# A causal convolution and a gated feed-forward layer: how the first x is loaded, how the taps are spread, and what TensorE does meanwhile

## The chip, the core and the metric

The kernel runs on one core of a Trainium2 chip. The metric is the device time of one execution in microseconds (us). The engines are TensorE (PE in the profile; PEld is its loading of stationary operands), VectorE (DVE), ScalarE (ACT), GpSimd (POOL) and SyncE (SP), which here issues transfers.

## The reference

`x` is 8 sequences of 4096 tokens with 192 channels. Each channel is convolved along the tokens with 7 taps; the channels fall into 8 heads of 24, and a head's taps are the softmax of its row of `weight`. The result goes through a feed-forward layer with a gate:

```python
w = weight - np.max(weight, axis=-1, keepdims=True)      # 8 heads x 7 taps
w = np.exp(w)
w = w / (np.sum(w, axis=-1, keepdims=True) + 1e-09)
x_pad = np.concatenate([np.zeros((B, pad, D), dtype=np.float32), x], axis=1)
idx = np.arange(S)[:, None] + np.arange(K)[None, :]
x_unf = x_pad[:, idx, :].reshape(B, S, K, H, group)
out = np.einsum('hk,bskhg->bshg', w, x_unf)              # 8 x 4096 x 192
...
gate = np.maximum(x @ w_gate, 0.0)                       # 192 -> 1536
val = x @ w_val
return (gate * val @ w_out).astype(np.float32)           # 1536 -> 192
```

## The kernel before

The tokens are worked in 16 units of 1024 tokens of two streams (sequence b and sequence b + 4), which lie in the two halves of the partitions. For each unit the convolved x (`xc`, channels on partitions, three chunks of 64 channels) is multiplied with `Wg` and `Wv` in 12 steps of 128 columns (`gate_val`, L477, matmuls L490). ScalarE applies the ReLU (L499), VectorE the product (L500), and `project` multiplies with `Wo` (L519, L539) and writes the rows out (L552, L553). The convolution of units 2 to 15 runs on VectorE, ScalarE and GpSimd beside the matmuls of earlier units. That of units 0 and 1 is done on PE, as a product with banded matrices that hold the taps: `conv_dense` for the two windows of 512 tokens of unit 0, `conv` for unit 1. The change touches what comes before the first `gate_val`.

The order of each engine's instructions is that of the program (`manual_schedule`), so an instruction that waits holds all that are behind it on its engine.

**The first x.** A window has five steps (`GSUB`) of 104 tokens, with six earlier tokens each. SyncE loads the taps' logits `wr` (L104), then steps 1 to 4 of the first stream as fp32 (L125) and step 0 of both streams (L141) into `stage`, which is a view of a buffer that is used only later (`prods`). GpSimd loads steps 1 to 4 of the second stream with a cast to fp16 straight into the tile `xts[0]` (L130). ScalarE casts the staged steps 1 to 4 (L275), VectorE step 0 (L276).

**The weights.** GpSimd issues their transfers in slices (`load_w`, L173) with a cast, into partitions 0 to 63. `both_halves` copies a slice to partitions 64 to 127 (L180): VectorE does it for slices 0 and 1, GpSimd for the others. Between slices 2 and 3 GpSimd issues the x of the second window (L90).

**The taps and the band.** VectorE takes the maximum (L214), ScalarE exp (L217), VectorE the sum, the reciprocal and the taps in `w8`, each repeated 16 times (L219 to L222). A matmul with a piece of the identity (L232) brings them onto 112 partitions (`spread`), VectorE multiplies with `same` (L242), and 14 matmuls with shifted `places` (L253) make the banded matrices of the eight heads in two PSUM tiles. `same` and `places` are sums over `spaced` (L201), which GpSimd fills (L129, L131). VectorE copies heads 0 to 3 to `band0`, ScalarE heads 4 to 7 to `band4` (both L282). Ten small transfers on SyncE lay the taps out on the partitions (L269) for the later units; GpSimd copies them on (L605).

**Filling matmuls.** `warm_up` (L155) multiplies constants into a PSUM tile that nobody reads: six matmuls of 512 columns at the start and two after `spread`.

**The first convolution.** `conv_dense(0, c)` for the three chunks c (L599) does 40 matmuls each (L318) over all five steps and copies the chunk to `xc` (L328): chunk 1 by VectorE, chunks 0 and 2 by ScalarE. Chunk 0 needs heads 0 to 2, chunk 1 heads 2 to 5, chunk 2 heads 5 to 7. Three more calls, for the second window, lie in the first `gate_val` (L482).

Of the kernel before, what the change touches and what calls it, by code (L numbers as in the profile page):

```python
# [15 lines left out]
def kernel(  # L16
# [98 lines left out]

    xts[0] = xpool.tile([128, GSUB, 2, D], F16, name="x_h")

    def body(st):
        return bass.AP(
            tensor=x.tensor,  # L120
            offset=x.offset + (NB * st * S + DSUB - PAD) * D,
            ap=[[D, SUB], [DSUB * D, GSUB - 1], [1, D]],
        )
# [6 lines left out]
    nc.gpsimd.dma_start(out=xts[0][0:SUB, 1:GSUB, 1, :], in_=body(1))  # L130
# [24 lines left out]
    def warm_up(count):  # L155
        for n in range(count):
            nc.tensor.matmul(
                out=warm[:, n % 2, :], lhsT=busy[:, 0:128], rhs=busy, start=True, stop=True
            )

    warm_up(6)

# [23 lines left out]
    load_w(0)  # L186
    load_w(1)
    load_w(2)
    xts[1] = load_x(1)
    load_w(3)  # L190
    pool_halves(2)
    load_w(4, 6)
    pool_halves(3)
# [25 lines left out]
    nc.vector.tensor_reduce(out=sm[:], in_=ex[:], axis=mybir.AxisListType.X, op=ALU.add)  # L219
    nc.vector.reciprocal(sm[:], sm[:])  # L220
    w8 = const.tile([H, KW, SEG], FP)
    nc.vector.tensor_scalar(  # L222
        out=w8[:],
        in0=ex[:, 0:KW].unsqueeze(2).to_broadcast([H, KW, SEG]),
        scalar1=sm[:],
        scalar2=None,
        op0=ALU.mult,
    )
# [3 lines left out]
    nc.tensor.matmul(  # L232
        out=spread[0:SUB, 0, 0:H],
        lhsT=w8[:].rearrange("h k s -> h (k s)"),
        rhs=spaced[0:H, 0, GAP : GAP + H],
        start=True,
        stop=True,
    )
    warm_up(2)
    diag = const.tile([SUB, H, SEG], F16)  # L240
    with nc.allow_low_precision("products with one and zero"):
        nc.vector.tensor_tensor(  # L242
# [2 lines left out]
            in1=same[:].unsqueeze(1).to_broadcast([SUB, H, SEG]),  # L245
            op=ALU.mult,
        )
    summed(places[:, SUB - SEG : SUB - SEG + SEG + KW - 1], pitch_k - 1, SEG + KW - 1, GAP)
    bps = psum.tile([128, 2, 512], FP, name="ps")
    HB = H // 2  # L250
    for a in range(2):
        for b in range(NSEG):
# [6 lines left out]
                skip_group_check=True,  # L259
            )  # L260

    taps = const.tile([H, KW], FP)
    nc.scalar.copy(out=taps[:], in_=w8[:, :, 0])
    tap = const.tile([128, NCH, KW], FP)
    for h in range(H):
        r = G * h
# [5 lines left out]
            )  # L272
            r += n

    nc.scalar.copy(out=xts[0][0:ROWS0, 1:GSUB, 0, :], in_=stage(0, ROWS0, 0, 1, 1, GSUB - 1))  # L275
    nc.vector.tensor_copy(out=xts[0][0:ROWS0, 0, :, :], in_=stage(0, ROWS0, 0, 2, 0, 1))  # L276

    bands = []
    for a, copy in ((0, nc.vector.tensor_copy), (1, nc.scalar.copy)):
        part = const.tile([128, HB, SUB], F16, name=f"band{a}")  # L280
        bands += [part[0 : SUB + PAD, h, :] for h in range(HB)]
        copy(  # L282
            out=part[:].rearrange("p h (b s) -> p h b s", s=SEG),
            in_=(bps, spread)[a][:, a, 0 : HB * SUB].rearrange("p (b h s) -> p h b s", h=HB, s=SEG),
        )

    def band(h):
        return bands[h]

    xc = {}  # L290

# [5 lines left out]
    def conv_dense(g, c):  # L297


        xt = xts[g]  # L300
        if g == 0 and c == 0:
# [5 lines left out]
        ps = psum.tile([128, 2, 512], FP, name="ps")  # L307
        for jj in range(GSUB):
            col = DSUB * jj
            n = min(DSUB, WIN - col)  # L310
            for second in range(2):
                for st in range(2):
                    for k2 in range(2):
                        k = 2 * c + k2
                        h0, h1 = 32 * k // G, (32 * k + 31) // G
                        h, m = (h0, G * h1 - 32 * k) if second else (h1, 32)
                        p0 = 64 * st + 32 * k2
                        nc.tensor.matmul(  # L318
                            out=ps[p0 : p0 + m, 0, col : col + n],
                            lhsT=xt[0:rows, jj, st, 32 * k : 32 * k + m],  # L320
                            rhs=band(h)[0:rows, 0:n],
                            start=True,
                            stop=True,
                            tile_position=(0, p0),
                            skip_group_check=True,
                        )
        copy = nc.vector.tensor_copy if c == 1 else nc.scalar.copy
        copy(out=xc[0][:, c, t0 : t0 + WIN], in_=ps[:, 0, :])  # L328

# [147 lines left out]
    def gate_val(u, w):  # L477
        h = hpool.tile([128, NFF, 2, WIN], F16, name="hT")
        xcb = xc[u]
        for f in range(NFF):  # L480
            if u == 0 and w == 0 and f in (5, 7, 9):
                conv_dense(1, (f - 5) // 2)  # L482
            pss = [psum.tile([128, 2, 512], FP, name="ps") for _ in range(2)]
            order = [(i, c) for i in range(2) for c in range(NCH)]
            if u == 0 and w == 0 and f == 0:
                order = [(0, 0), (0, 1), (1, 0), (0, 2), (1, 1), (1, 2)]
            for i, c in order:
                W = (Wg, Wv)[i]
                for st in range(2):
                    nc.tensor.matmul(  # L490
                        out=pss[i][:, st, :],
                        lhsT=W[64 * st : 64 * st + 64, c, 128 * f : 128 * (f + 1)],
                        rhs=xcb[64 * st : 64 * st + 64, c, WIN * w : WIN * (w + 1)],
                        start=(c == 0),
                        stop=(c == NCH - 1),
                        tile_position=(64 * st, 0),
                    )
# [179 lines left out]
```

## Time and profile before

| | us |
|---|---|
| three runs | 769.77, 771.62, 771.74 |
| their median | 771.62 |
| the profiled execution | 769.56 |
| its span, from the first instruction to the last | 767.9 |
| busy: PE, VectorE, ScalarE, GpSimd | 761.8, 685.1, 604.1, 369.8 |
| first matmul of L490 | 8.10 |
| last matmul of L519 ends | 764.15 |

The profile is of one execution. Its page gives busy time by engine and by group of instructions; the trace behind it can be asked for all instructions in order of time, for the chain of waits (from the last instruction back to what released each step) and for transfers. A row of the timeline reads: start, length, engine, line, operation, output and inputs, shapes, how many, and in brackets how long the engine stood idle before it and what ended that.

### The profile page before, as it was taken

Reading aid. Unit: us, or ns where it says so; the run is one execution under the profiler, and the core shown is the slowest. Engines: PE = TensorE matmul, PEld = TensorE weight load, DVE = VectorE, ACT = ScalarE, POOL = GpSimd, SP = SyncE. Lnnn points to the kernel's source line nnn. Section 1 sums busy time; section 2 is a strip of 40 time slices with the busy share of each in tenths; the row PEclk is TensorE's granted clock in tenths of the full one; section 3 lists DMA queues with packets and bytes.
Section 4 is the critical chain, followed back from the end, with each engine's and each line's share of the span. In section 5 each row is a group of like instructions: output and inputs, shape, how many; then the busy total and the mean of one; then the engine's idle time right before and its main releaser. Section 6 shows DMA issues by size and latency. Waiting matters only on the chain.

```text
span 767.9 us, 24835 instructions
## 1 busy us (share of the span) xinstructions
PE 761.8 (99%) x10840; PEld 526.8 (69%) x10840; DVE 685.1 (89%) x728; ACT 604.1 (79%) x733; POOL 369.8 (48%) x212
## 2 busy tenths in 40 slices
PE   8999999999999999999999999999999999999998
PEld 4495675957759576585866858567595775957757
DVE  6999999989999999999999999999998999995590
ACT  6788887888878788887888878788787887874571
POOL 8608738093470925619166290843909346090000
PEclk9999999999999999999999999999999999999999
DMA  8946727180372704529064271712819231200102
GB/s 121 133 101 118 91 88 91 48 126 7 100 78 69 106 23 94 63 85 94 23 110 48 85 91 44 109 27 85 93 44 114 24 94 38 65 21 23 63 2 84
DMA packets 131809, 56.11 MB, mean 73 GB/s; under 512 B 96741, under 2 KB 131701, under 8 KB 131701
## 3 DMA queue, kind: packets, MB, share of 16 engines
q1 hardware_dynamic: 90789, 38.85, 24.3%
q0 software_dynamic: 40768, 15.59, 18.9%
q8 instruction: 84, 1.38, 0.8%
q14 instruction: 24, 0.20, 0.1%
q10 hardware_dynamic: 144, 0.10, 0.0%
HBM read 31.68 MB, written 25.17 MB: 74 GB/s over the span
## 4 chain that ended last, share of the span: by engine, by line
PE 99%; DMA 0%; DVE 0%; SPq 0%; issue 0%
PE ps L490 65%; PE ps L519 31%; PE ps L539 2%; DMA prods<-in_x_dram 0%; PE ps L318 0%; PE ps L343 0%; DVE xc L328 0%; DVE x_h L276 0%; DVE band L282 0%; SPq L104 0%; DVE acc L552 0%; SPq L125 0%
## 5 line engine op out<-in xcount | busy, mean ns | idle before, releaser
L500 DVE TENSOR_TENSOR hT<-gr,ps 128x1024 f16<-128x1024 f16 x384 | 468.4, 1221 | 59.9 <-ACT gr L499 32.2
L499 ACT ACTIVATE gr<-ps 128x1024 f16<-128x1024 f32 x384 | 393.0, 1023 | 100.5 <-PE ps L490 100.4
L443 POOL TENSOR_TENSOR prods<-prods 128x1344 f32<-128x1344 f32 x70 | 212.4, 3034 | 309.4 <-ACT out_s L552 279.3
L490 PE MATMUL ps<-xc,Wg 64*128 64x512 f16 x2304 | 317.3, 376 | 0.1
L490 PE MATMUL ps<-xc,Wv 64*128 64x512 f16 x2304 | 317.1, 376 | 0.0
L519 PEld LDWEIGHTS <-hT 64*128 64x128 f16 x5760 | 238.5, 94 | 3.1
L519 PE MATMUL ps<-Wo,hT 64*128 64x192 f16 x5760 | 240.3, 243 | 0.0
L490 PEld LDWEIGHTS <-Wv 64*128 64x128 f16 x2304 | 138.6, 94 | 111.0 <-issue 2.9
L490 PEld LDWEIGHTS <-Wg 64*128 64x128 f16 x2304 | 128.1, 94 | 116.6 <-issue 0.6
L466 DVE SCALAR_TENSOR_TENSOR acc<-x_r,tap,acc 128x576 f32<-128x576 f16 x210 | 154.3, 811 | 1.6 <-ACT acc L454 1.6
L437 ACT ACTIVATE prods<-x_r,tap 128x448 f32<-128x448 f16 x222 | 130.2, 660 | 1.2 <-DMA x_r<-x_p 1.2
L552 ACT COPY out_s<-ps 128x768 f32<-128x768 f32 x63 | 50.3, 799 | 53.1 <-PE ps L519 44.5
L399 POOL DMA_DIRECT2D x_e<-in_x_dram x56 | 45.2, 819 | 3.3 <-POOL x_p L418 3.3
L418 POOL COPY x_p<-x_e 128x1728 f16<-128x1728 f16 x28 | 44.7, 1621 | 2.4 <-DMA x_e<-in_x_dram 2.4
L443 POOL TENSOR_TENSOR xc<-prods 128x1344 f16<-128x1344 f32 x14 | 42.4, 3028 | 1.1
L466 DVE SCALAR_TENSOR_TENSOR xc<-x_r,tap,acc 128x576 f16<-128x576 f16 x42 | 31.8, 811 | 0.0
L454 ACT ACTIVATE acc<-x_r,tap 128x576 f32<-128x576 f16 x42 | 29.4, 767 | 0.0
L439 DVE TENSOR_SCALAR prods<-x_r,tap 128x448 f32<-128x448 f16 x72 | 27.3, 448 | 0.0
L539 PE MATMUL ps<-Wo,hT 128*128 128x192 f16 x192 | 16.2, 246 | 0.0
L539 PEld LDWEIGHTS <-hT 128*128 128x128 f16 x192 | 15.9, 98 | 0.0
L552 DVE COPY acc<-ps 128x192 f32<-128x192 f32 x1 | 0.4, 359 | 14.2 <-PE ps L519 14.2
L90 POOL DMA_DIRECT2D x_h<-in_x_dram x6 | 4.9, 826 | 0.0
(51 smaller groups left out, 56.4 us busy)
## 6 DMA issues: line engine op xcount, KB each, us to landing
out_dram<-out_s SPq DMA_DIRECT2D x63, 384.0 KB
x_e<-in_x_dram POOLq DMA_DIRECT2D x34, 192.0 KB, 6.6
x_e<-in_x_dram POOLq DMA_DIRECT2D x22, 240.0 KB, 6.3
x_r<-x_p SPq DMA_TRANSPOSE x126
Wo<-in_moe_w_out_dram POOLq DMA_DIRECT2D x1, 576.0 KB, 10.7
x_h<-in_x_dram POOLq DMA_DIRECT2D x2, 240.0 KB, 8.2
x_h<-in_x_dram POOLq DMA_DIRECT2D x2, 210.0 KB, 5.2
x_h<-in_x_dram POOLq DMA_DIRECT2D x2, 192.0 KB, 5.8
```

What stands on the lines that cost most here:

```text
L399: nc.gpsimd.dma_start(out=xe[:, j : j + n, st, :, :].rearrange("p j c r -> p j (c r)"), in_=bass.AP(tensor=x.tensor, offset=x.offset + (b ...
L418: nc.gpsimd.tensor_copy(out=xp[:, :, :, st, :], in_=xe[:, :, st, :, :])
L437: engine.activation(out=out, in_=in_, func=ACTF.Copy, scale=scale)
L443: nc.gpsimd.tensor_tensor(out=pr[:, 0] if k < KW - 1 else xc[u][:, :, LDVE:UNIT], in0=pr[:, 0], in1=pr[:, k], op=ALU.add,)
L454: nc.scalar.activation(out=accs[u][:, c, :], in_=shifted(u, c, 0, 0), func=ACTF.Copy, scale=tap[:, c, 0:1],)
L466: nc.vector.scalar_tensor_tensor(out=xc[u][:, c, 0:LDVE] if k == KW - 1 else acc[:, c, :], in0=shifted(u, c, k, 0), scalar=tap[:, c, k : k ...
L490: nc.tensor.matmul(out=pss[i][:, st, :], lhsT=W[64 * st : 64 * st + 64, c, 128 * f : 128 * (f + 1)], rhs=xcb[64 * st : 64 * st + 64, c, WI ...
L499: nc.scalar.activation(out=gr[:], in_=pss[0][:], func=ACTF.Relu)
L500: nc.vector.tensor_tensor(out=h[:, f], in0=gr[:], in1=pss[1][:], op=ALU.mult)
L519: mm = nc.tensor.matmul(out=outs[q], lhsT=h[64 * r : 64 * r + 64, f, st, 128 * q : 128 * (q + 1)], rhs=Wo[64 * r : 64 * r + 64, f, :], sta ...
L539: nc.tensor.matmul(out=outs[q], lhsT=h[:, f, st, 128 * q : 128 * (q + 1)], rhs=Wo[:, f, :], start=(f == 0), stop=(f == NFF - 1),)
L552: copy(out=dst, in_=src if len(src.shape) == 3 else src.unsqueeze(1))
```

## The change

- SyncE loads all of the first x as fp32: step 1 of both streams, step 0 of both streams, then steps 2 to 4 of the first and of the second stream. GpSimd's cast transfer is gone.
- GpSimd copies the maximum of the logits (`lead`) before it issues the first weights.
- exp writes each value 16 times at once, and is the stationary operand of the `spread` matmul as it is; the moving operand is the piece of the identity divided by the sum (`over`). `taps` is scaled by the reciprocal on ScalarE. The sum for `places` stands ahead of the product.
- VectorE copies the band in two parts (heads 0 to 2, head 3), ScalarE heads 4 to 7 as before. ScalarE casts step 1 of both streams, VectorE step 0; after the band ScalarE casts steps 2 to 4 of the first stream and VectorE those of the second.
- `conv_dense` for the first window runs in two rounds over the three chunks: steps 0 and 1, then steps 2 to 4.
- Filling matmuls: six of 512 columns and one of 128 at the start; 256 and 192 columns after `spread`; one of 512 after the 14 matmuls of the band.

```diff
-    nc.sync.dma_start(out=stage(0, SUB, 0, 1, 1, GSUB - 1), in_=body(0))
+    FEW = 2
+    rest = [DSUB * D, GSUB - FEW]
+    nc.sync.dma_start(out=stage(0, SUB, 0, 2, 1, 1), in_=body(1, [NB * S * D, 2]))
...
-    nc.gpsimd.dma_start(out=xts[0][0:SUB, 1:GSUB, 1, :], in_=body(1))
...
+    for st in range(2):
+        nc.sync.dma_start(
+            out=stage(0, SUB, st, 1, FEW, GSUB - FEW), in_=body(FEW, rest, st)
+        )
...
-    warm_up(6)
+    warm_up(512, 512, 512, 512, 512, 512, 128)
...
-    ex = const.tile([H, KW + 1], FP)
+    ex = const.tile([H, KW + 1, SEG], FP)
...
-    nc.scalar.activation(ex[:, 0:KW], wr[:], ACTF.Exp, bias=mx[:])
+    lead = const.tile([H, 1], FP)
+    nc.gpsimd.tensor_copy(out=lead[:], in_=mx[:])
+    load_w(0)
...
+    nc.scalar.activation(
+        ex[:, 0:KW, :], wr[:].unsqueeze(2).to_broadcast([H, KW, SEG]), ACTF.Exp, bias=mx[:]
+    )
...
-    w8 = const.tile([H, KW, SEG], FP)
+    over = const.tile([H, H], FP)
     nc.vector.tensor_scalar(
-        out=w8[:],
-        in0=ex[:, 0:KW].unsqueeze(2).to_broadcast([H, KW, SEG]),
+        out=over[:],
+        in0=spaced[0:H, 0, GAP : GAP + H],
         scalar1=sm[:],
...
     summed(same[:], pitch_k, SEG, GAP)
+    summed(places[:, SUB - SEG : SUB - SEG + SEG + KW - 1], pitch_k - 1, SEG + KW - 1, GAP)
...
-        lhsT=w8[:].rearrange("h k s -> h (k s)"),
-        rhs=spaced[0:H, 0, GAP : GAP + H],
+        lhsT=ex[:, 0:KW, :].rearrange("h k s -> h (k s)"),
+        rhs=over[:],
...
-    warm_up(2)
+    warm_up(256, 192)
...
-    summed(places[:, SUB - SEG : SUB - SEG + SEG + KW - 1], pitch_k - 1, SEG + KW - 1, GAP)
...
+    warm_up(512)
+
     taps = const.tile([H, KW], FP)
-    nc.scalar.copy(out=taps[:], in_=w8[:, :, 0])
+    nc.scalar.activation(taps[:], ex[:, 0:KW, 0], ACTF.Copy, scale=sm[:])
...
-    nc.scalar.copy(out=xts[0][0:ROWS0, 1:GSUB, 0, :], in_=stage(0, ROWS0, 0, 1, 1, GSUB - 1))
+    nc.scalar.copy(out=xts[0][0:ROWS0, 1, :, :], in_=stage(0, ROWS0, 0, 2, 1, 1))
...
+    fill_band(0, [0, 1, 2], nc.vector.tensor_copy)
+    fill_band(1, [4, 5, 6, 7], nc.scalar.copy)
+    fill_band(0, [3], nc.vector.tensor_copy)
+    nc.vector.tensor_copy(
+        out=xts[0][0:ROWS0, FEW:GSUB, 1, :], in_=stage(0, ROWS0, 1, 1, FEW, GSUB - FEW)
+    )
+    nc.scalar.copy(
+        out=xts[0][0:ROWS0, FEW:GSUB, 0, :], in_=stage(0, ROWS0, 0, 1, FEW, GSUB - FEW)
+    )
...
-    for c in range(NCH):
-        conv_dense(0, c)
+    pieces = [psum.tile([128, 2, 512], FP, name="ps") for _ in range(NCH)]
+    for steps in (range(FEW), range(FEW, GSUB)):
+        for c in range(NCH):
+            conv_dense(0, c, pieces[c], steps)
```

In the changed kernel the three new SyncE transfers of x stand in lines 127 and 149, `lead` in 214, VectorE's cast of steps 2 to 4 in 305, and the two rounds of the convolution use line 342 for its matmuls.

More of the change, by code (lines that the diff above doesn't have):

```diff
@@ L116, with body @@
     xts[0] = xpool.tile([128, GSUB, 2, D], F16, name="x_h")
-    def body(st):
+    def body(jj, step, st=0):
         return bass.AP(
             tensor=x.tensor,
-            offset=x.offset + (NB * st * S + DSUB - PAD) * D,
-            ap=[[D, SUB], [DSUB * D, GSUB - 1], [1, D]],
-        )
-    nc.sync.dma_start(out=stage(0, SUB, 0, 1, 1, GSUB - 1), in_=body(0))
+            offset=x.offset + (NB * st * S + DSUB * jj - PAD) * D,
+            ap=[[D, SUB], step, [1, D]],
+        )
+    FEW = 2
+    rest = [DSUB * D, GSUB - FEW]
+    nc.sync.dma_start(out=stage(0, SUB, 0, 2, 1, 1), in_=body(1, [NB * S * D, 2]))
     ones = const.tile([128, SUB], FP)
@@ L153, with warm_up @@
     warm = psum.tile([128, 2, 512], FP, name="ps")
-    def warm_up(count):
-        for n in range(count):
+    def warm_up(*widths):
+        for n, w in enumerate(widths):
             nc.tensor.matmul(
-                out=warm[:, n % 2, :], lhsT=busy[:, 0:128], rhs=busy, start=True, stop=True
+                out=warm[:, n % 2, 0:w], lhsT=busy[:, 0:128], rhs=busy[:, 0:w], start=True, stop=True
             )
-    warm_up(6)
+    warm_up(512, 512, 512, 512, 512, 512, 128)
     Wg = const.tile([128, NCH, DFF], F16)
@@ L184, in pool_halves @@
         both_halves(nc.gpsimd.tensor_copy, s, Wv)
[L186 to L193, printed above, removed]
-    ex = const.tile([H, KW + 1], FP)
+    ex = const.tile([H, KW + 1, SEG], FP)
     nc.vector.memset(ex[:], 1e-9)
@@ L216 @@
     )
-    nc.scalar.activation(ex[:, 0:KW], wr[:], ACTF.Exp, bias=mx[:])
+    lead = const.tile([H, 1], FP)
+    nc.gpsimd.tensor_copy(out=lead[:], in_=mx[:])
+    load_w(0)
+    load_w(1)
+    load_w(2)
+    xts[1] = load_x(1)
+    load_w(3)
+    pool_halves(2)
+    load_w(4, 6)
+    pool_halves(3)
+    nc.scalar.activation(
+        ex[:, 0:KW, :], wr[:].unsqueeze(2).to_broadcast([H, KW, SEG]), ACTF.Exp, bias=mx[:]
+    )
     sm = const.tile([H, 1], FP)
-    nc.vector.tensor_reduce(out=sm[:], in_=ex[:], axis=mybir.AxisListType.X, op=ALU.add)
+    nc.vector.tensor_reduce(out=sm[:], in_=ex[:, :, 0], axis=mybir.AxisListType.X, op=ALU.add)
     nc.vector.reciprocal(sm[:], sm[:])
-    w8 = const.tile([H, KW, SEG], FP)
+    over = const.tile([H, H], FP)
     nc.vector.tensor_scalar(
-        out=w8[:],
-        in0=ex[:, 0:KW].unsqueeze(2).to_broadcast([H, KW, SEG]),
+        out=over[:],
+        in0=spaced[0:H, 0, GAP : GAP + H],
         scalar1=sm[:],
@@ L273, with fill_band @@
             r += n
-    nc.scalar.copy(out=xts[0][0:ROWS0, 1:GSUB, 0, :], in_=stage(0, ROWS0, 0, 1, 1, GSUB - 1))
+    nc.scalar.copy(out=xts[0][0:ROWS0, 1, :, :], in_=stage(0, ROWS0, 0, 2, 1, 1))
     nc.vector.tensor_copy(out=xts[0][0:ROWS0, 0, :, :], in_=stage(0, ROWS0, 0, 2, 0, 1))
[L278 to L281, printed above, removed]
+    band_at = {}
+    def fill_band(a, heads, copy):
+        lo, n = heads[0] - HB * a, len(heads)
+        part = const.tile([128, n, SUB], F16, name=f"band{heads[0]}")
+        for i, h in enumerate(heads):
+            band_at[h] = part[0 : SUB + PAD, i, :]
         copy(
             out=part[:].rearrange("p h (b s) -> p h b s", s=SEG),
-            in_=(bps, spread)[a][:, a, 0 : HB * SUB].rearrange("p (b h s) -> p h b s", h=HB, s=SEG),
-        )
+            in_=(bps, spread)[a][:, a, 0 : HB * SUB].rearrange("p (b h s) -> p h b s", h=HB, s=SEG)[
+                :, lo : lo + n
+            ],
+        )
+    fill_band(0, [0, 1, 2], nc.vector.tensor_copy)
[7 more added lines that the diff above has]
+    )
     def band(h):
-        return bands[h]
+        return band_at[h]
     xc = {}
@@ L295, with conv_dense @@
     PLACE |= {6: (1, 0, 0), 7: (1, 0, 1), 2: (1, 1, 0), 5: (1, 1, 1)}
-    def conv_dense(g, c):
+    def conv_dense(g, c, ps, steps=range(GSUB)):
         xt = xts[g]
-        if g == 0 and c == 0:
+        if g == 0 and c == 0 and 0 in steps:
             xc[0] = xcpool.tile([128, NCH, UNIT], F16, name="xc")
@@ L306, in conv_dense @@
         rows = ROWS0
-        ps = psum.tile([128, 2, 512], FP, name="ps")
-        for jj in range(GSUB):
+        for jj in steps:
             col = DSUB * jj
@@ L326, in conv_dense @@
                         )
+        if GSUB - 1 not in steps:
+            return
         copy = nc.vector.tensor_copy if c == 1 else nc.scalar.copy
@@ L481, in gate_val @@
             if u == 0 and w == 0 and f in (5, 7, 9):
-                conv_dense(1, (f - 5) // 2)
+                conv_dense(1, (f - 5) // 2, psum.tile([128, 2, 512], FP, name="ps"))
             pss = [psum.tile([128, 2, 512], FP, name="ps") for _ in range(2)]
```

## The prediction

> **What bounds the kernel now.** I read the page's busy times first, then the chain of waits, then the opening microseconds engine by engine. PE is busy 761.8 of 767.9 us, and the chain of waits (start us, length us, what) shows why nothing but the opening can matter:
>
> ```profile
> 1.68 3.75 DMA prods<-in_x_dram
> 5.43 0.02 issue
> 5.45 0.54 DVE x_h L276
> 5.99 0.54 DVE band L282
> 6.53 0.04 issue
> 6.57 1.26 PE ps L318 x80
> 7.84 0.02 issue
> 7.86 0.70 DVE xc L328
> 8.56 0.04 issue
> 8.61 6.61 PE ps L490 x58
> ...
> 748.28 15.87 PE ps L519 x384
> ```
>
> From 8.61 to 764.15 us the chain is PE work alone. The change edits only what stands before 8.61, so a microsecond there is a microsecond of the whole, and no more than about 8 us is in play. The chain before it: the second of SP's transfers of x (L141, landed 5.43), VectorE's cast of it (L276), VectorE's copy of band 0 to 3 (L282), two thirds of the 120 matmuls of the first convolution, the copy of its chunk 1, then the dense stage. The timeline of PE shows how it spends that time:
>
> ```profile
> 0.86 2.72 PE L157 MATMUL ps<-const-bfloat16-1.0 128*128 128x512 bf16 x6 [0.86 <-PEq L661]
> 3.53 0.52 PE L232 MATMUL ps<-spaced,w 8*112 8x8 f32 x2
> 3.98 0.66 PE L157 MATMUL ps<-const-bfloat16-1.0 128*128 128x512 bf16 x2
> 4.78 0.58 PE L253 MATMUL ps<-diag,places 112*128 112x64 f16 x14
> 6.57 1.59 PE L318 MATMUL ps<-band,x_h 110*32 110x104 f16 x120 [1.21 <-DVE band L282]
> ```
>
> Two things are to be seen. PE has nothing to do for 1.2 us from 5.36. And the first six filling matmuls take 2.72 us, some 0.42 us each (0.2 us of tail taken off, the length of a single small matmul of L318), while the next two take 0.66, some 0.23 each: in this execution PE doubled its rate at about 4 us.
>
> The opening's transfers, in 40 slices of 0.2 us (DMA share and GB/s of the first 8 us):
>
> ```profile
> DMA  0000000000054359999999999999999999999999
> GB/s 0 0 0 0 0 0 0 0 1 1 0 42 42 61 100 315 372 365 376 355 301 221 179 196 184 194 162 156 151 159 183 177 175 197 174 165 180 150 146 185
> ```
>
> Five rows of the timeline of all engines that the sum uses (start, length, engine, line; the transfers' lengths are those of their issues):
>
> ```profile
> 1.43 0.88 POOL L130 DMA_DIRECT2D x_h<-in_x_dram  x1 [0.28 <-issue]
> ...
> 2.67 0.68 POOL L173 DMA_DIRECT2D Wg<-in_moe_w_gate_dram  x1
> ...
> 3.07 0.32 DVE L222 TENSOR_SCALAR w<-ex,sm 8x112 f32<-8x112 f32 x1
> ...
> 4.29 0.43 DVE L201 TENSOR_REDUCE places<-spaced 112x22 f16<-112x154 f32 x1
> ...
> 4.86 0.83 ACT L275 CAST x_h<-prods 110x768 f16<-110x768 f32 x1 [1.24 <-DMA prods<-in_x_dram]
> ```
>
> The slices say that SP's fp32 transfers run alone until about 4 us at some 370 GB/s; then GpSimd's casting ones come in and the total is 180.
>
> **Times.** The profiled execution took 769.56 us, of which 767.9 are the span and 1.66 lie around it. The three runs gave 769.77, 771.62 and 771.74. So the four times stand in two pairs, about 769.7 and 771.7, two microseconds apart. The sum is made against 769.56; the median, 771.62, belongs to the other pair, and what makes the pair is half of this forecast.
>
> **SP's x, L127, L141, L149.** GpSimd's cast transfer (L130, 0.88 us to issue, 168 KB written) goes; SP carries 168, 156, 252 and 252 KB in place of 336 and 156. By the slices 49 kB have moved at 3.0 us, and 0.372 kB per ns from there. The old first transfer (344 kB) is through at 3.8 and its reader (ACT L275) starts at 4.86; the old second (504 kB in all, partly beside casts) is through at some 4.5 and landed 5.43: 1.0 us of lag in both. With 172, 332, 590 and 848 kB of running total the new ones are through at 3.3, 3.75, 4.45 and 5.15 and land at 4.3, 4.75, 5.45 and 6.15. The last meets the first weights: their issue ends at 3.35, as before, and the first cast transfer's packets came 1.6 us after the end of its own issue (2.31 to 3.9), so from 4.9. If the last 92 kB get half of 190 GB/s they are through at 5.9 and land 6.9. If there is less lag or no hindrance, 5.85. I take 6.15: only the tail meets the weights. The issues cost SP two more of 0.34 us (L125's row), done by 2.9; behind them on SP wait the ten transfers of the taps, which started at 3.64 and are first needed on GpSimd at 19.97, the last issue ending at 11.4: 8 us of cover.
>
> **GpSimd.** Without L130 the select (L131, 0.36) ends about 1.8 in place of 2.74. The new copy of mx waits for VectorE (2.34) and ends about 2.6, so the weights' issues begin at 2.6 where they began at 2.67: nothing. All GpSimd's work is queued behind that copy; the first weights landed before 6.5 and are now copied by VectorE after 7.0, half a microsecond of cover, which is the price if mx comes late.
>
> **The taps.** exp on 8x112 instead of 8x7 adds 105 elements at some 0.9 ns (ACT: 448 in 0.53, 1024 in 1.02): +0.09. `over` on 8x8 instead of 112 columns costs 0.15 (VectorE's small rows) and not 0.32: -0.17. The spread matmul can't start before the fillers end (3.4 plus 128 columns, 3.5), where it started anyway: nothing until 4.05. `places` (0.43) now runs ahead of the product (L242, ends 4.37) and not behind it, so the 14 matmuls start at 4.42 and not 4.78: -0.36, and they end 5.0.
>
> **First piece.** VectorE casts step 0 from 4.77 to 5.31, copies three heads of band (336 of 448 columns: 0.47 of 0.60) to 5.77, PE starts at 5.82 in place of 6.57; head 3 follows to 6.0, ACT has heads 4 to 7 at about 5.6. 48 matmuls of 120 end at 6.4. A gain of 0.75, if the rest could follow.
>
> **Second piece.** It can't: VectorE must cast steps 2 to 4 of the second stream, 576 columns, 1.5 times L276: 0.82 by ratio, 0.74 by its slope, 0.78 taken. From 6.17 to 6.95; PE goes on at 7.0. ACT's 576 of the first stream lie between 5.6 and 6.3, hidden. Then 48 of the 80 matmuls of the chain (1.06 x 0.6 + 0.2 = 0.84) to 7.84, the copy of chunk 1 at 7.86, dense stage at 8.61. The sum is 0.0: what band and step 0 gain, the last transfer takes back. Ends: 5.85 lets VectorE go on without a wait, -0.3; 6.9 gives +0.75. The two weight copies of VectorE (0.28 and 0.56) move behind the cast, to 7.8, just ahead of the chunk's copy: hidden by 0.05, 0.3 if GpSimd slows them more.
>
> **Fillers.** Seven for six, 448 columns for 1024, one new of 512 before the first piece. None is on the chain at full rate. But they decide how long PE stands still: at half rate the 14 matmuls end near 5.4, the filler at 5.6, the first piece runs 5.8 to 6.9, the second starts 7.0. Holes of about 0.2 and 0.1 us replace 1.0 or more. This bears on the pairs: if PE doubled its rate late, the 1.43 us of the first convolution takes 2.86, its chunk 1 is copied about 0.9 us later, and half the time from there to the doubling is lost; a doubling at 11.7 us gives the 2.0 us between the pairs. That a hole puts off the doubling is my assumption; the pairs and the two rows of L157 fit it, no row proves it. With it, all executions of the new kernel come out with the lower pair.
>
> The Trainium skill (TensorE: Matmul & The Clock Gate, Part 1: The HAM clock gate) says that the array runs at half its clock until a window of some 3.4 us, running freely against the kernel's start, has been busy. The rows of L157 agree with a doubling near 4 us; how busy is busy enough it does not say, and if the short holes count as busy, an estimate from that window (0.86 plus two of them) has the doubling before 7.7 us, the same 769.6; if they don't, it is rival B.
>
> **Forecast (A, 0.57).** The median joins the lower pair: 769.56 + 0.0, rounded to 769.5 us. Its own range is 768.9 to 770.3: the ends of the second piece, -0.3 and +0.75, with 0.3 more below for the 0.2 us by which two runs of one pair differ and the 0.04 of VectorE's cast.
>
> **Rivals.** **B (0.15): the fillers do nothing for the pairs.** They come from something else, or the hole at 6.4 to 7.0 does what that at 5.4 did. Then 771.6, as before. For it: no view shows an execution of the upper pair. Against: 2 us is just what a late doubling costs.
> **C (0.17): the x lands early.** Sharing with the weights is slight and the lag is that of a queue without casts, 5.85 or less: VectorE never waits, -0.3: 769.2, less when its cast takes 0.74: 769.1. For it: the 1.0 of lag is measured with casts in the engines. Against: 828 KB at 372 GB/s don't end before 5.1.
> **D (0.11): slower.** The engines' shared rate, 180 GB/s, holds all along, since the four SP transfers and the weights overlap more than I think: 800 kB after 3.0 take 4.4 us, landing 8.4. The second piece starts at 9.25, dense 10.86, +2.25: 771.8, over the median before; PE stands still nearly 3 us and the doubling may go late as well, +2.0: 773.8 and more. It decides from a landing of about 8 us. Against: SP alone had 370.
>
> **Chances.** 0.3%, 2.3 us, is about what a measurement of this kernel can tell from no change; against 771.62 its lower edge is 769.3, inside A. Faster: C and 45% of A (0.26), 0.43. Slower (over 773.9): 0.08 of D. Within: 0.49. Range 768.6 to 772.1: leaves out the upper D and the far ends of C and A.
>
> **What would show it.** The first piece should start near 5.8 and end at 6.4; VectorE's cast L305 should start at the landing, 6.2; dense stage within 0.4 of 8.6. Wrong if: the landing comes after 7, the fillers' row shows two rates later than 6.5 us, or the new kernel's times still stand two microseconds apart.

## The result, and the profile after

| | us |
|---|---|
| before, 8 runs | 770.58 median (769.77 to 771.74) |
| after, 8 runs | 773.55 median (773.02 to 774.80) |
| ratio, with its 95% interval | 1.0041 [1.0030, 1.0052] |
| profiled execution after, its span | 773.04, 771.1 |

The changed kernel is slower by 0.41%, three microseconds, and the forecast of 769.5 (768.6 to 772.1) did not hold. The chain of waits of the changed kernel (start us, length us, what), up to the dense stage:

```profile
2.15 0.39 SPq L149
2.53 0.04 issue
2.58 5.07 DMA prods<-in_x_dram
7.65 0.02 issue
7.67 0.76 DVE x_h L305
8.44 0.04 issue
8.48 1.09 PE ps L342 x48
9.57 0.04 issue
9.60 8.17 PE ps L516 x60
```

Before, the chain went through the second of two SP transfers, which landed at 5.43; now it goes through the last of four, issued by 2.53 and landed at 7.65. VectorE's cast of steps 2 to 4 follows it at once, then the second piece of the convolution, then the dense stage. The last line has a second thing to show: 60 matmuls take 8.17 us, where the chain before had 58 in 6.61. PE's timeline shows both:

```profile
5.80 0.81 PE L342 MATMUL ps<-band,x_h 110*32 110x104 f16 x48
7.27 0.22 PE L342 MATMUL ps<-band,x_h 110*32 110x104 f16 x2 [0.66 <-ACT x_h L308]
8.48 1.09 PE L342 MATMUL ps<-band,x_h 110*32 110x104 f16 x70 [0.99 <-DVE x_h L305]
9.60 1.09 PE L516 MATMUL ps<-xc,Wg 64*128 64x512 f16 x4
10.46 0.66 PE L516 MATMUL ps<-xc,Wv 64*128 64x512 f16 x2
...
13.71 0.82 PE L516 MATMUL ps<-xc,Wg 64*128 64x512 f16 x6
```

The first piece starts at 5.80 (5.82 was forecast). Then PE stands still for 0.66 and 0.99 us in place of one hole of 1.21. And the dense matmuls of 512 columns cost more at 10.46 than at 13.71: two take 0.66 and six take 0.82, some 0.23 us for each of two against 0.10 for each of six once the tail of 0.2 is taken off. PE works there at half its rate. Two windows of 3.4 us of the same kernel (window; its length, then the busy us of PE, PEld, DVE, ACT, POOL with instructions in brackets; granted clock; DMA share; GB/s):

```profile
5.83:9.25 3.42, 1.77 (x118) 1.47 (x119) 1.24 (x3) 1.14 (x3) 3.38 (x6) 1.00 1.29 151
9.25:12.66 3.41, 3.37 (x34) 1.37 (x27) 2.15 (x4) 1.91 (x3) 3.00 (x5) 0.50 1.41 159
```

In the first, PE has work for 1.77 us only, with its clock at 1.00; in the second, which is full of dense matmuls, the clock is 0.50. (Until the rate first rises the column shows 1.00 too, while the filling matmuls run at half rate, so it is read only after that.) The doubling had come in time, at 5.83, and was taken back.

The transfers of the first 8 us, in slices of 0.2 us, and the two kinds of queue:

```profile
DMA  0000000000033999895579898999999999999999
GB/s 0 0 0 0 0 0 0 0 0 1 0 42 88 265 365 334 288 296 131 131 250 276 280 234 273 264 256 238 232 210 168 182 179 170 170 126 97 124 139 134
...
q1 hardware_dynamic: 1280, 0.85, 38.8%
q0 software_dynamic: 919, 0.34, 38.3%
```

The rate falls to 131 at 3.6 to 4.0 us, about where the third of SP's transfers begins (0.34 MB have moved by 3.6, and the first two hold 0.33), and then stays at 230 to 280 until 5.8, where the forecast's sum had SP's x moving at 372 until 5. Until 5.05 this is SP's x alone: only then does the first packet of GpSimd's queue come, close to the 4.9 of the forecast. In the whole 8 us GpSimd's queue moved 0.34 MB and held the engines as long as SP's queue did for 0.85 MB.

**Where the 3.2 us between the two spans went (767.9 to 771.1).** The first dense matmul moved from 8.10 to 9.60, +1.50. From there to the first product of the second unit's band on PE (L343, now L369: starts 41.81 and 44.32) it took 33.71 before and 34.72 after, +1.01: the half rate. From there to PE's last matmul (764.15 and 766.99), +0.33, nearly all of it at one place late in the kernel:

```profile
673.10 0.80 ACT L578 COPY out_s<-ps 128x768 f32<-128x768 f32 x1 [0.94 <-ACT prods L463]
```

ScalarE stands still for 0.94 us before this copy; before the change it was 0.66 at the same copy (L552, 670.26). And behind PE's last matmul +0.36 (3.75 to 4.11). The experiments deal with the first two; the last two come and go with the kernel and stand at the end.

### The profile page after: what moved, and what is told of

Its sections match the earlier page's. It is cut to its first block, busy times and chain, and to the rows that moved or that the text cites. A ratio compares the mean times of both kernels' runs of the same rounds, so it can differ in the third digit from the quotient of the medians.

```text
span 771.1 us, 24846 instructions
## 1 busy us (share of the span) xinstructions
PE 764.3 (99%) x10842; PEld 527.6 (68%) x10842; DVE 686.2 (89%) x730; ACT 604.5 (78%) x734; POOL 369.3 (48%) x212
## 4 chain that ended last, share of the span: by engine, by line
PE 98%; DMA 1%; DVE 0%; issue 0%; ACT 0%; SPq 0%; ACTq 0%
PE ps L516 64%; PE ps L545 31%; PE ps L565 2%; DMA prods<-in_x_dram 1%; PE ps L342 0%; PE ps L369 0%; DVE hT L526 0%; ACT gr L525 0%; DVE x_h L305 0%; SPq L149 0%; DVE prods L141 0%; SPq L142 0%; DVE acc L578 0%; DVE ones L129 0%; DVE ex L192 0%
## 5 line engine op out<-in xcount | busy, mean ns | idle before, releaser
L342 PE MATMUL ps<-band,x_h 110*32 110x104 f16 (+7 forms) x240 | 4.0, 211 | 1.6 <-DVE x_h L305 1.0
```

## The experiments

The theory after this result, in three parts. (1) The last transfer of x lands late, and the dense stage follows it. (2) The holes it leaves on PE cost the rate. (3) It lands late through sharing with the weights, or through being the last of four, or for another reason. The rivals are named with each. All kernels but e3 are the changed kernel with the edit shown; e3 is the kernel before with one. The ratios are against the kernel before, measured beside each.

### e1: fill the hole in PE

```diff
         for c in range(NCH):
             conv_dense(0, c, pieces[c], steps)
+        if 0 in steps:
+            for _ in range(7):
+                nc.tensor.matmul(
+                    out=pieces[0][:, 1, :], lhsT=busy[:, 0:128], rhs=busy, start=True, stop=True
+                )
```

> The changed kernel with seven more filling matmuls of 512 columns between the first piece of the first convolution (steps 0 and 1) and the second. Theory (the last transfer of x is late, 7.65 us, and PE's standing still from 6.6 to 8.5 us makes its rate fall to half for 3.4 us): the dense stage still starts at about 9.6, the half-rate stretch after 9.25 is gone, and the time falls by about 1.5 us, from 773.5 to 772.0. Rival (the rate falls for another reason, or the filling matmuls do nothing for it): 773.5, and the stretch stays. Rival (seven are too many where they run at half rate): 774.

Measured: 772.77 us (772.21 to 775.26, 10 runs), ratio 1.0036 [1.0022, 1.0049]. PE's timeline:

```profile
5.50 0.77 PE L342 MATMUL ps<-band,x_h 110*32 110x104 f16 x48 [0.18 <-DVE band L295]
6.21 1.70 PE L631 MATMUL ps<-const-bfloat16-1.0 128*128 128x512 bf16 x7
7.84 0.22 PE L342 MATMUL ps<-band,x_h 110*32 110x104 f16 x2
8.58 0.98 PE L342 MATMUL ps<-band,x_h 110*32 110x104 f16 x70 [0.52 <-DVE x_h L305]
9.71 0.78 PE L516 MATMUL ps<-xc,Wg 64*128 64x512 f16 x4
10.31 0.39 PE L516 MATMUL ps<-xc,Wv 64*128 64x512 f16 x2
```

Two dense matmuls at 10.31 take 0.39 now, not 0.66: the rate stays. From the first dense matmul to L369 (43.25) it takes 33.54 in place of 34.72, so the half rate had cost 1.18. The landing stays (7.75). In the profiled executions part 2 holds: the hole took the rate, and the rate was worth 1.18. Of this gain the profiled execution gives back 0.78 after PE's last matmul (a tail of 4.89 against 4.11). The medians don't show it clearly: the ratios, 1.0036 and 1.0041, have intervals that overlap, and two of the ten executions took over 775, longer than any of the changed kernel. No profile shows why.

### e2: the first x as before, all else as changed

```diff
-    nc.sync.dma_start(out=stage(0, SUB, 0, 2, 1, 1), in_=body(1, [NB * S * D, 2]))
+    nc.sync.dma_start(out=stage(0, SUB, 0, 1, 1, GSUB - 1), in_=body(1, most))
...
+    nc.gpsimd.dma_start(out=xts[0][0:SUB, 1:GSUB, 1, :], in_=body(1, most, 1))
...
-    for st in range(2):
-        nc.sync.dma_start(
-            out=stage(0, SUB, st, 1, FEW, GSUB - FEW), in_=body(FEW, rest, st)
-        )
...
-    for steps in (range(FEW), range(FEW, GSUB)):
+    for steps in (range(GSUB),):
```

(With it go the casts of the parts and the two rounds of the convolution; ScalarE casts steps 1 to 4 of the first stream as before.)

> The changed kernel with the x transfers, their casts and the single round of the first convolution as before; the taps' chain, the band in three parts, GpSimd's copy of mx and the filling matmuls as changed. Theory (the x transfers by SyncE cost all of the loss): the dense stage starts at 8.4 to 8.7, no half-rate stretch, 769.7 to 770.6. Rival (the weights' later issue or the fewer filling matmuls cost it): 772 to 773.5.

Measured: 770.27 us (769.27 to 772.22, 10 runs), ratio 1.0001 [0.9988, 1.0015]. The way in which x is loaded, with its casts and rounds, carries the whole loss; the taps, `lead`, the parts of band and the fillers together are worth nothing that can be measured. The profiled execution (770.95) happens to be one in which the rate went up late, at 10.14:

```profile
6.68 2.75 PE L334 MATMUL ps<-band,x_h 110*32 110x104 f16 x120 [0.81 <-DVE band L293]
```

The same 120 matmuls took 1.59 us before, and the first dense one comes at 9.37. So the spread of the kernel before is still in this one, with 0.81 us of idle time ahead of the convolution.

### e3: the kernel before, with two more filling matmuls

```diff
                 skip_group_check=True,
             )
 
+    warm_up(2)
+
     taps = const.tile([H, KW], FP)
```

The place is behind the 14 matmuls of the band, in the 1.2 us for which PE had nothing to do.

> The kernel before with two more filling matmuls of 512 columns after the 14 matmuls of the band, where PE stood still for 1.2 us. Theory (the 2 us by which executions of the kernel before differ come from a rate that rises late when that hole falls into the span that decides it): its executions move together near 769.8, ratio 0.999. Rival (they differ for another reason): the same 769.8 to 771.7, ratio 1.000.

Measured: 769.66 us (769.53 to 769.90, 10 runs), ratio 0.9991 [0.9982, 1.0000], beside 25 runs of the kernel before on the same chip that lie anywhere from 769.29 to 772.71 (median 770.09). PE's timeline:

```profile
4.82 0.93 PE L253 MATMUL ps<-diag,places 112*128 112x64 f16 x14
5.58 0.60 PE L157 MATMUL ps<-const-bfloat16-1.0 128*128 128x512 bf16 x2
6.72 1.56 PE L320 MATMUL ps<-band,x_h 110*32 110x104 f16 x120 [0.54 <-DVE band L284]
8.21 0.88 PE L492 MATMUL ps<-xc,Wg 64*128 64x512 f16 x4
```

The dense stage starts no earlier than before (8.21 against 8.10), so these two matmuls shorten nothing where the rate rose in time anyway. They take away the slower executions: the ten times lie within 0.4 us where the kernel before spreads over 3.4. That those were executions with a late rise fits, and e2's profile shows one such, but no slower execution of the kernel before was profiled. This is the best kernel of the study, though by little in the median, with an interval that reaches 1.0000.

### e4 and e5: the weights earlier, and later

Earlier: GpSimd issues the first weights without waiting for the maximum, as the kernel before did (first issue at 1.75 in place of 2.53).

```diff
-    lead = const.tile([H, 1], FP)
-    nc.gpsimd.tensor_copy(out=lead[:], in_=mx[:])
     load_w(0)
```

> The changed kernel without GpSimd's copy of mx, so that the first weights are issued about 0.9 us earlier, at 1.65. Theory (the last transfer of x is late because it shares the DMA engines with the weights' casts): it lands later still, 8.2 or more, the dense stage starts after 10.1, 774 or more. Rival (it is late for a reason of its own): it lands at 7.6 as in the changed kernel, 773.5.

Measured: 774.63 us (773.91 to 775.61, 4 runs), ratio 1.0055 [1.0036, 1.0074]. The time holds a second loss, which the theory did not have: in the profiled execution the rate rises only at 14.68, and until then PE works at half of it, as in this row (0.98 in e1):

```profile
9.11 1.70 PE L340 MATMUL ps<-band,x_h 110*32 110x104 f16 x70 [1.54 <-DVE x_h L303]
```

Later: `lead` reads the diagonal of the taps, which is ready only at about 4.5, so that the weights' issues begin at 4.88.

```diff
-    lead = const.tile([H, 1], FP)
-    nc.gpsimd.tensor_copy(out=lead[:], in_=mx[:])
-    load_w(0)
...
+    lead = const.tile([H, 1], F16)
+    nc.gpsimd.tensor_copy(out=lead[:], in_=diag[0:H, 0, 0:1])
+    load_w(0)
```

> The changed kernel with GpSimd's small copy reading the product for the band (ready at about 4.5 us) in place of mx, so that the first weights are issued some 2.1 us later, at 4.65, and their packets come at about 6.8. What is read is when VectorE's cast of steps 2 to 4 of the second stream starts. Theory (sharing the DMA engines with the weights makes the last transfer late): 6.2 to 6.6 instead of 7.67. Rival (four transfers on SyncE's queue are slow by themselves): 7.4 or later. The time is not expected to gain, since the weights then bound the dense stage: 771 to 774.

Measured in one execution: 771.26 us. VectorE's row of the cast in the two kernels, the one with the early weights first:

```profile
8.31 0.75 DVE L303 CAST x_h<-prods 110x576 f16<-110x576 f32 x1 [2.19 <-DMA prods<-in_x_dram]
```

```profile
7.18 0.75 DVE L305 CAST x_h<-prods 110x576 f16<-110x576 f32 x1 [1.55 <-DMA prods<-in_x_dram]
```

Against 7.67 in the changed kernel, it is 0.64 later with the early weights and 0.49 earlier with the late ones. That is the theory's direction, but a difference of this size between two executions is not clear of chance: e6 and e7 below have the same transfers and land 0.61 apart. In e5 the landing lies between the theory's 6.6 and the rival's 7.4. The packets say more: there the first packet of GpSimd's queue comes at 6.43, and still the last packet of x ends only at 6.58 (6.95 in the changed kernel) and the last x lands at 7.16, a microsecond behind the forecast's 6.15. Sharing does cost rate where it happens: from 3.6 to 5.0 us SP's queue moved 0.18 MB in e4, whose weights come from 3.76, and 0.31 in the changed kernel, whose weights come from 5.05. But it can't be the main cause of a delay that is there without the weights. In e5 the first dense matmul comes at 9.11, earlier by the same 0.49, and runs at full rate: part 1 again.

### e6 and e7: steps 2 to 4 of the second stream by GpSimd, without and with fillers

GpSimd loads this piece with a cast at the place where it did before, and VectorE's cast of it goes; SP has three transfers. The second kernel has two filling matmuls between the pieces as well, as in the first experiment.

```diff
+    nc.gpsimd.dma_start(out=xts[0][0:SUB, FEW:GSUB, 1, :], in_=body(FEW, rest, 1))
...
-    for st in range(2):
-        nc.sync.dma_start(
-            out=stage(0, SUB, st, 1, FEW, GSUB - FEW), in_=body(FEW, rest, st)
-        )
+    nc.sync.dma_start(
+        out=stage(0, SUB, 0, 1, FEW, GSUB - FEW), in_=body(FEW, rest)
+    )
```

> The changed kernel with steps 2 to 4 of the second stream loaded by GpSimd with a cast, ahead of the select and the weights, straight into the fp16 tile (no VectorE cast of them); all else as changed, the two pieces too. Theory: the transfer lands by about 6, ScalarE's cast of the first stream's steps ends by 6.8, the second piece starts by 7.0 and the dense stage by 8.4: 769.5 to 770.2. Rival (the two pieces with a hole between them cost, whoever loads x): 771 or more.

> The kernel of the run before with two more filling matmuls of 512 columns between the two pieces. Theory: as it, without the executions whose rate rises late or falls: median 769.2 to 769.6, all within 0.5 us. Rival (the hole is too short to matter): as the run before.

Measured: 771.75 us (770.06 to 773.88, 9 runs), ratio 1.0019 [1.0004, 1.0034], and with fillers 771.05 (770.24 to 771.95, 10 runs), ratio 1.0008 [0.9999, 1.0018]. ScalarE's row in the first:

```profile
7.37 0.67 ACT L305 CAST x_h<-prods 110x576 f16<-110x576 f32 x1 [1.43 <-DMA prods<-in_x_dram]
```

In the changed kernel ScalarE cast its part at 6.54. Now SP's third transfer, the last of its queue, lands at 7.34 (7.95 in the kernel with fillers, which has the same transfers), and the dense stage starts at 9.35. So the lateness is not that of one range of x or of VectorE: the transfer that is now the last on SP is late in its turn, with GpSimd's casting transfer on the same engines. The half rate is in the first (8.57 to 11.99) and not in the second. Both theories missed: e6's time is the rival's, and the rate that e7 kept did not bring it to 769.2 to 769.6, since its x landed later still.

### e8: the fourth transfer on ScalarE's queue

```diff
-    for st in range(2):
-        nc.sync.dma_start(
-            out=stage(0, SUB, st, 1, FEW, GSUB - FEW), in_=body(FEW, rest, st)
-        )
+    nc.sync.dma_start(
+        out=stage(0, SUB, 0, 1, FEW, GSUB - FEW), in_=body(FEW, rest)
+    )
...
+    nc.scalar.dma_start(
+        out=stage(0, SUB, 1, 1, FEW, GSUB - FEW), in_=body(FEW, rest, 1)
+    )
```

> The changed kernel with the last transfer of x (steps 2 to 4 of the second stream) issued by ScalarE right after exp, at about 2.8 us, where SyncE issued it at 2.6. Theory (the engines are shared, whichever queue feeds them): it lands at 7.2 to 7.9 and the time stays at 773 to 774. Rival (it is late since it stands fourth on SyncE's queue): it lands before 6.6 and the time falls by 1 us or more.

Measured: 774.07 us (772.34 to 775.18, 8 runs), ratio 1.0046 [1.0032, 1.0061]. ScalarE's row:

```profile
8.77 0.67 ACT L310 CAST x_h<-prods 110x576 f16<-110x576 f32 x1 [2.76 <-DMA prods<-in_x_dram]
```

SP's third transfer, now the last of SP's x, landed at 8.75 and ScalarE's at 9.10. The completions of the third on the 16 engines were all in by 6.90 but one; the last engine brought 8.75. Both landings are later than theory and rival had. A second queue doesn't help, and a transfer lands with its slowest engine.

### e9 and e12: three transfers in place of four, and then with late weights

Step 0 of both streams first, then steps 1 to 4 of each stream; the same bytes, one cast less, and the convolution in one round.

```diff
-    nc.sync.dma_start(out=stage(0, SUB, 0, 2, 1, 1), in_=body(1, [NB * S * D, 2]))
+    most = [DSUB * D, GSUB - 1]
...
-            out=stage(0, SUB, st, 1, FEW, GSUB - FEW), in_=body(FEW, rest, st)
+            out=stage(0, SUB, st, 1, 1, GSUB - 1), in_=body(1, most, st)
```

> The changed kernel with all x by SyncE as fp32 in three transfers in place of four: step 0 of both streams first, then steps 1 to 4 of the first stream, then those of the second; the first convolution in one round. Read are the start of VectorE's cast of the second stream's steps and the packets of 768 bytes that take over 150 ns. Theory (many of the packets are slow wherever a range of x is first read while others wait in line behind them): slow packets after 3.2 us again, and the last x lands at 7.2 or later. Rival (the cutting into four transfers makes it late): it lands before 6.6. Time 772 to 774 either way, since nothing is done with step 1 early.

Measured in one execution: 771.80 us. VectorE's row:

```profile
6.78 0.92 DVE L304 CAST x_h<-prods 110x768 f16<-110x768 f32 x1 [1.15 <-DMA prods<-in_x_dram]
```

The last x lands 0.9 us earlier, at 6.76 (between the rival's 6.6 and the theory's 7.2, near the rival), and its 16 engines complete within 0.26 us of one another (6.50 to 6.76), where the last transfer of the changed kernel had them from 5.89 to 7.65. PE, left with longer holes, lost its rate (7.74 to 11.15), which takes the gain back.

The last run puts the two halves together: e9's transfers, the late weights, and three filling matmuls of 512 columns ahead of the first convolution.

```diff
-    lead = const.tile([H, 1], FP)
-    nc.gpsimd.tensor_copy(out=lead[:], in_=mx[:])
...
+    lead = const.tile([H, 1], F16)
+    nc.gpsimd.tensor_copy(out=lead[:], in_=diag[0:H, 0, 0:1])
...
-    warm_up(512)
+    warm_up(512, 512, 512)
```

> The three transfers of the run before (step 0, then steps 1 to 4 of each stream) with the first weights issued about 2.1 us later, and three filling matmuls of 512 columns instead of one ahead of the first convolution. The question is whether the two parts of the late landing add up: the cutting into four was worth 0.89 us (7.65 to 6.76), the weights 0.49 (7.65 to 7.16). If they are separate: the last x lands near 6.3, VectorE's cast (0.93) ends near 7.2, the convolution goes on at 7.25 and the dense stage begins near 8.4; the profiled execution takes about 769.4 if PE keeps its rate. If both only relieve the same slow engines: landing 6.6 to 6.8, dense stage 8.7 to 8.9, 769.7 to 769.9. PE's idle time from 5.9 to the landing plus 1.0 is some 1.4 us in a window of 3.41, so the rate should stay full by the rows so far (windows with 1.94 to 2.11 us of work kept it, those with 1.78 or less lost it), and the executions should lie close together, within 1 us; if they spread over 2 us or more, the windows do not decide it.

Measured: 770.65 us (770.10 to 771.19, 10 runs), ratio 1.0004 [0.9994, 1.0014]. The landing is 6.56 (the cast starts at 6.58): 0.2 earlier than with three transfers alone, not 0.5. That the two halves add up is not shown; 0.2 is within what two executions of the same transfers differ by. PE kept its rate, but the profiled execution (770.78) is 0.9 over what was expected, for the chain of waits now goes elsewhere:

```profile
5.58 2.45 DMA Wv<-in_moe_w_val_dram
8.03 0.02 issue
8.05 0.29 DVE Wv L185
8.34 0.03 issue
8.37 0.70 DVE xc L353
9.07 0.04 issue
9.12 6.61 PE ps L515 x58
```

Weights that are issued late land late: VectorE's copy of the first of `Wv` waits until 8.03 and holds the copy of the convolved chunk behind it on VectorE, so the dense stage enters the chain at 9.12 in place of 8.61. No kernel here reached the forecast's landing of 6.15.

### e10 and e11: two that did not do what they should

**e10 is e2 with three filling matmuls** of 512 columns in place of one:

```diff
-    warm_up(512)
+    warm_up(512, 512, 512)
```

> The changed kernel with x as before (as in the run that undid it) and three filling matmuls of 512 columns in place of one after the 14 matmuls of the band. Theory (a hole of PE decides when its rate rises): all executions near 769.6 and within 0.5 us, median at or just below that of the kernel before with its hole filled. Rival (the executions of the run that undid x differed for another reason): 769.3 to 772.2 again.

Measured: 770.36 us (769.59 to 771.39, 10 runs), ratio 0.9996 [0.9985, 1.0008]. The times draw together less than expected (within 1.8 us, not 0.5). The profiled execution (771.39) holds its rate and its PE ends at 764.26, 0.1 behind the kernel before; but the span goes on for 5.4 us behind that, where the kernel before has 3.75. In this tail lies a fetch of code, which the kernel before doesn't have there. It is no explanation: seven other kernels have one there too, with tails of 3.7 to 4.9 us. So a part of the spread can come from the end of the kernel; this one execution doesn't show how much.

**e11 touches the ranges of x first**, by two small transfers of ScalarE (32 bytes of every eighth row), against the theory that the first read of a range is slow:

```diff
+    for st in range(2):
+        nc.scalar.dma_start(
+            out=touch[0:14, st],
...
+                ap=[[8 * D, 14], rest, [1, 8]],
+            ),
+        )
```

> The changed kernel with two small transfers by ScalarE at the start, ahead of all else on its queue, that read 32 bytes of every eighth row of the ranges that the last two transfers of x read later. The taps come about 0.8 us later. Theory (the slow packets are first reads of a range): of the 14 packets of 768 bytes that took over 150 ns after 3.2 us at most 5 are left, and the last x lands before 6.8. Rival (they are slow for another reason, such as many transfers in line): 10 or more, landing 7.3 or later.

Measured in one execution: 773.16 us, landing 8.12. In the packet records a packet of 768 bytes mostly takes 36 ns; nine that began after 3.2 us took over 150 here, one of them 1159, against 14 in the changed kernel (to 695) and none in the kernel before. The number lies between the theory's five and the rival's ten, and the landing is the rival's: a first touch of this kind doesn't bring x earlier. (The rate rose late here as well, at 12.42, so the time says little about the landing.)

## Why the prediction was wrong

**SP's x: the step that failed.** "I take 6.15: only the tail meets the weights." It measured 7.65. The prediction laid the four transfers behind one another at the 372 GB/s that two of them had shown, added 1.0 us of lag, and looked for the danger in the weights. The term that was mis-sized is the rate of the four transfers themselves. From 3.6 to 5.0 us no packet of GpSimd's queue is on the engines yet, and SP's queue moved this (packets, MB, share of 16 engines) in the changed kernel, in e5 and in e9:

```profile
q1 hardware_dynamic: 428, 0.31, 81.8%
...
q1 hardware_dynamic: 447, 0.33, 89.0%
...
q1 hardware_dynamic: 604, 0.45, 104.0%
```

That is 225 GB/s in the changed kernel and 323 with three transfers. By 5.0 us 0.65 MB had moved; the forecast's own rate gives 0.79. The last packet of x ended at 6.95 and not at 5.15; with the weights out of the way (e5) at 6.58, and with three transfers at 5.94. So most of the delay lies in how the four transfers move, and a smaller part, not measured clear of chance, in the weights. The lag was not the fault: 0.70 us from the last packet to the landing (0.73 before).

The profiled kernels with four transfers on SP landed at 7.16 to 8.28 (changed kernel, e1, e4, e5, e11), those with three of the same bytes at 6.76 and 6.56 (e9, e12). A landing is that of the slowest of 16 engines, and with four transfers single engines fall behind: in e1 14 of them are done by 6.81 and the last at 7.75, in e5 15 by 6.70 and the last at 7.16. What makes an engine fall behind stays open: the queue (e8), the range (e6) and the first read (e11) were tried, and none of them explains it.

**Second piece.** The working from the landing on was right: cast at once, 0.76 for 0.78, PE on 0.04 us later, then the dense stage (the chain goes there straight from the 48 matmuls and not over VectorE's copy of chunk 1). Put in 7.65 for 6.15 and it gives the +1.50 of the first dense matmul. One bound was mis-added: by the prediction's own rows VectorE is busy until 6.0, so a landing at 5.85 would gain 0.17 and not 0.3. Nothing hung on it.

**Fillers: the second step that failed, as a consequence.** "Holes of about 0.2 and 0.1 us" were 0.66 and 0.99. The assumption that a hole decides about the doubling, which no row proved, is borne out by e3: with the hole filled all ten executions lie from 769.53 to 769.90, near the lower end of the kernel before. What the prediction did not think of is that the rate, once doubled, can be taken back. The trace's records of the granted clock begin with the first rise, and a fall comes one window of 3.41 us later in four kernels. These are the windows ahead of the fall, or after the rise where none came (PE's busy us in it):

| kernel | window | PE busy | the next window |
|---|---|---|---|
| fourth transfer on ScalarE (e8) | 5.94 to 9.36 | 0.67 | half |
| three transfers (e9) | 4.33 to 7.74 | 1.49 | half |
| changed kernel | 5.83 to 9.25 | 1.77 | half |
| GpSimd's piece (e6) | 5.16 to 8.57 | 1.78 | half |
| kernel before | 4.13 to 7.54 | 2.06 | full |
| late weights (e5) | 4.13 to 7.54 | 2.11 | full |
| GpSimd's piece with fillers (e7) | 4.33 to 7.74 | 2.15 | full |
| three transfers, late weights (e12) | 4.61 to 8.02 | 2.36 | full |

The windows of the kernel that lost its rate with the most work, e6, and of the one that kept it with the least, the kernel before (columns as above):

```profile
5.16:8.57 3.41, 1.78 (x99) 1.34 (x100) 1.35 (x4) 1.21 (x2) 3.41 (x6) 1.00 1.30 164
8.57:11.99 3.42, 3.42 (x62) 1.63 (x48) 1.98 (x3) 1.88 (x3) 3.06 (x5) 0.50 1.37 158
```

```profile
4.13:7.54 3.41, 2.06 (x102) 1.52 (x104) 2.44 (x6) 1.55 (x3) 3.41 (x6) 1.00 1.47 179
7.54:10.95 3.41, 3.29 (x76) 1.85 (x65) 1.87 (x4) 2.31 (x4) 3.37 (x6) 1.00 1.29 141
```

In e3, e10 and e1 the window had 2.77 to 3.23, and the rate stayed. So in these eleven executions the border lies between 52% and 60% of a window. The Trainium skill (TensorE: Matmul & The Clock Gate, Why this matters for your kernels) asks that no gap between bursts of matmuls be longer than about 3 us, and has the clock fall after an idle window. The length agrees roughly (the half rate lasted 3.41 us here); the condition is stricter in these runs, where holes of 0.66 and 0.99 us in one window were enough.

The first rise asks for much more than keeping the rate. In these eleven executions it came at 4.13 to 5.95 us, each time at the end of a window with 3.27 us of work (kernel before, e5) or 3.41 (the others). In e2, e11 and e4 it came only at 10.14, 12.42 and 14.68. Counted back from there, the windows that did not raise it had 2.60 us in e2, 2.63 and 2.39 in e11, and in e4 3.13 (a wait of 0.28 us at 3.69), 3.14 (PE out of work for the last 0.27) and 2.16. The middle one of these, and the one that raised it:

```profile
4.44:7.85 3.41, 3.14 (x68) 2.13 (x67) 1.43 (x4) 1.20 (x2) 3.41 (x6) 1.00 1.30 224
...
11.27:14.68 3.41, 3.41 (x20) 1.23 (x18) 2.22 (x3) 1.20 (x2) 3.26 (x5) 1.00 0.90 110
```

So here 92% of a window was too little and 96% enough. The windows begin at another place in each execution, as the rises from 4.13 to 5.95 show, so that a hole of the opening spoils one in some executions and not in others. This fits the spread of the kernel before; it rests on one profiled execution of each kernel.

**The rivals.** D was right in its outcome: a late landing moves the dense stage, and the rate goes as well. Its mechanism was not right, since it had the weights share the engines all along and they come at 5.05. It was said to decide from a landing of about 8 us; 7.65 was enough, since the prediction put the loss of the rate only on an idle time of nearly 3 us. C is out: x landed late. Of B the first half is out, since the fillers do bear on the spread (e3); its second half, that the hole between the pieces costs what the old one did, came near, though by a fall and not by a late rise.

**The taps, GpSimd, the first piece** came near the forecast: the 14 matmuls start at 4.54 for 4.42, the weights' issues at 2.53 for 2.6, the first piece at 5.80 for 5.82. The last agreement is partly luck: VectorE cast step 0 in 0.36 us and not 0.54, and PE had the 14 matmuls and the filling matmul behind them at half rate until then; where the rate rose by 4.54 (e1, e5, e7, e9) the first piece starts at 5.50. All this was worth nothing that can be measured (e2: all of it without the transfers is 1.0001), and in the changed kernel the second piece waits for the landing alone.

**The two pairs of times.** With eight and then 25 runs they are no pairs but a spread from 769.3 to 772.7. That a hole in the opening makes it is shown by e3 for the kernel before, and a late rise as the way is seen in e2's profile alone. e10 spreads over 1.8 us with its hole filled; for that only the long end of one execution is known.

## What to carry to other kernels

When a load is cut into more transfers so that the first work can start sooner, the end of the chain is set by the slowest engine of the last piece: take the rate and the landing of the last of several from a trace with as many transfers, and not from one with fewer (372 GB/s for two; 225 for four, from 3.6 to 5.0 us). Where PE must wait at the start of a long dense stage, count the waiting time in windows of 3.4 us and fill it, nearly all of it until the rate has risen and over 60% afterwards: two matmuls that nobody reads were worth more here (769.66, all within 0.4 us) than a redesign of the load. And what a change gains ahead of a wait that ends last is worth nothing until that wait ends sooner.

## What was not expected of the hardware

- The clock fell after a window in which PE was busy for half the time, and stayed at half for one window of 3.41 us; that cost 1.0 to 1.2 us.
- To rise for the first time the clock wanted a window that was nearly full: 3.27 of 3.41 us raised it, 3.14 did not (e4, which rose at 14.68).
- Four transfers on one queue moved at 225 GB/s where three of the same bytes moved at 323 (3.6 to 5.0 us, no packets of another queue beside them). Why is open.
- A transfer of 16 engines can complete 1.8 us behind its 15th engine (e8: 6.90 and 8.75).
- ScalarE stands still for 0.94 us before its copy near 672 us in the changed kernel, e1, e4, e5, e6 and e7, and for 0.66 in the other kernels, with the same work around it. It costs PE 0.3 us. Its cause was not tried; nothing near that place was edited.
- Behind PE's last matmul the span goes on for 3.6 to 4.1 us in most kernels, 4.9 in e1 and 5.4 in e10, and what lies around the span was 1.66 us before, 1.94 after and 2.48 in e12. So a microsecond won at the start can be hidden by one at the end, and a single execution doesn't show it.
